# Attention block on one core: two of four x blocks by transposing DMAs, second queries projected ahead of the exps, first bound rows on VectorE, planner tables set to uniform values

## The chip, the core and the metric

The kernel runs on one core of a Trainium2 chip. The metric is device time in microseconds (us) of one execution. Three executions of the kernel before took 406.65 to 406.67 us, median 406.66 us. One core has a matrix engine (PE, with PEld its weight loads), VectorE (DVE), ScalarE (ACT), GpSimd (POOL), and SyncE (SP), which here only issues DMAs.

## The reference

```python
qkv = (x @ wqkv).reshape(B, S, 3, H, Dh).transpose(2, 0, 3, 1, 4)   # B=1 S=2048 D=448 H=16 Dh=28
scores = einsum("bhqd,bhkd->bhqk", q, k) * Dh ** -0.5
p = softmax(scores, axis=-1)
o = einsum("bhqk,bhkd->bhqd", p, v)
out = o.transpose(0, 2, 1, 3).reshape(B, S, D) @ wo                 # all bf16
```

## The kernel before, in words

**Tiles.** The 2048 rows of x are four blocks of 512. Sixteen heads are four groups of four. A window is one group with one block of queries: 16 windows, each of 16 key tiles (128 keys) by 4 heads. A tile is one head's 128 keys by 512 queries, and there are 1024 tiles of scores (L941, `emit_S`).

**Softmax work is shared.** ACT takes pairs of tiles from the two-bank tiles `PA` (L1370, one exp of 128x1024). DVE takes single tiles from the banks `PD` with a cubic in place of the exp: DU (L1145), DV (L1148), then POOL's DG (L1151), then PTD (L1164). A few tiles ("early" ones, read ahead of their turn) are copied by DVE to SG (L1077) and computed by POOL alone (L1084 to L1107). PE then multiplies by the values (L1209) into `PO`.

**Bounds.** Instead of a running maximum, each score has a bound subtracted, carried in extra rows of queries and keys: the absolute queries QP times the largest absolute key. For the first two windows (w = 0 and 1) only key block 0 is known, so their first four key tiles use rows made on chip (`bound`, L749 to L757; `PBND` says which rows POOL makes, the others are DVE's). The later key tiles need all four key blocks projected, their maxima (L593, L636), the row NK (L641), and DMAs that move the keys into place (L647) and repeat NK beside them (L658).

**Start.** Block b of x must stand transposed in XT. Blocks 0 to 2 are loaded (XS, L303) and transposed by PE (L463), then copied out of the banks (L474, L476). Block 3 comes by four transposing DMAs (L310), the first of which waits for XS of block 1. Weights are loaded by L300 (WK, from ACT's queue), L307 (WQ), L314 (WV) and padded (L426 on POOL, L427 on ACT). POOL clears VA and WO (L497, L498) ahead of L426. Queries of window 0 and keys of block 0 are projected (L720, L584), reduced, moved and bounded, and then the first exp runs. The second queries (w = 1) and the other keys are projected between the first exps.

**What sets the order.** A list scheduler inside the kernel (L1402 to L1486) simulates the five engines with durations written in the file, and emits every instruction in the order that it finds. `XLAT` and the `lat=` of the SP items tell it when loads land; `prio`, `elig` and `acq` say what goes first, when, and into which bank. `PLAN` (L45 to L69) holds one number per window for many of its choices: how many ready rows start a window's value products, how far ahead an early tile is taken, priorities of DU, DV, PTD, and when projections may start and must be done. In the kernel before these numbers differ from window to window. Each engine then runs its own list in order; a wait at the head of a list stops all that stands behind it.

Of the kernel before, what the change touches and what calls it, by code (L numbers as in the profile page):

```python
# [13 lines left out]
ALU = mybir.AluOpType  # L14
# [31 lines left out]
    "PVROWS": [8, 10, 10, 3, 6, 7, 11, 7, 7, -10, 7, 7, 11, 11, 11, 9],  # L46
    "AHEAD": [16, 9, 16, 15, 7, 10, 12, 8, 12, 13, 11, 6, 13, 7, 11, 5],
    "GCLEAR": [0.4, -0.4, -0.3, 0.3, 0.2, 0.7, 0.3, -0.1, 0.2, 1, 0.5, 1, 0.4, 0.8, 1.4, 0.1],
    "SCLEAR": [0, 1.1, 1.8, 1.7, 1.4, 0.4, 0.7, 0, 0.3, 1.5, 0.1, 0.9, 1.8, 2, 0.4, 1.8],
# [6 lines left out]
    "QBY": [64, 33, 84, 35, 80, 63, 48, 35, 70, 68, 37, 26, 24, 83, 73, 82],
    "QLEAD": [-88, 27, 38, -61, -3, -56, 48, 32, 6, -83, 0, 17, 28, -85, -90, 11],
    "KFROM": [34, 11, 29, -12, -10, -8, 19, 19, 18, 30, 41, -14, 27, 26, 8, 2],
    "KBY": [23, 12, 48, -4, 29, 50, 40, 54, 30, -2, 2, 49, 14, 48, 9, 40],
    "KLEAD": [34, 27, -74, -63, -7, -50, 32, 24, 1, -25, -43, -62, 18, -27, -8, 47],  # L60
    "VFROM": [-2, 8, 7, 30, -2, 49, 8, 15, 40, -1, -5, 24, 46, -9, 35, 43],
    "VBY": [41, 25, 52, 0, 56, 14, 11, 57, 57, 37, 59, 4, 57, -8, 17, 49],
    "VLEAD": [48, 73, 0, -21, 9, -23, 6, 54, 46, 20, 21, -27, -34, 9, -21, -1],
    "NORM": [20, 10, -10, 38, 6, 40, 20, 10, -14, -4, 9, -10, -18, 20, 32, -1],
    "TAIL": [8, 8, 40, 1],
    "PART": [-34, -19, 34, 37, -30, 40, 3, 30],
    "OUT": [0, 10, 28, 39, 20, -22, 7, -6, 5, -8, -2, 39, -30, -10, 13, 39],
    "SLK": [0.2, 0.22, 0.21, 0.19, 0.12, 0.21, 0.2, 0.12, 0.24, 0.11, 0.08, 0.22, 0.17, 0.19, 0.27, 0.12],
# [49 lines left out]
def kernel(  # L118
# [87 lines left out]
    BP2 = 34  # L206
    PBND = ((3,), (2, 3))
# [10 lines left out]
    XT3 = 14.0  # L218
    XBAR = True
# [4 lines left out]
    out_perm = out[0][QW:S].rearrange("(p t) d -> p t d", t=NKT - TPC)  # L224
    out_last = out[0][0:QW].rearrange("(t p) d -> p t d", t=TPC)
    x_perm = x2[QW:S].rearrange("(p t) c -> p t c", t=NKT - TPC)
# [6 lines left out]
    def sb(shape, dt, name):  # L233
        return const.tile(shape, dt, name=name)

    XT = [[sb([CK + 2 * hf if b < NQC - 1 else P, 2, QW], BF16, f"XT{b}_{hf}") for hf in range(2)] for b in range(NQC)]
# [15 lines left out]
    XS = [sb([P, TPC, D], BF16, f"XS{b}") for b in range(NQC - XBAR)]  # L252
# [46 lines left out]
    xs_dma = []  # L299
    nc.scalar.dma_start(out=WK[:, :, 0:GW], in_=wq3[:, :, D:D + GW])  # L300
    for b in range(NQC):
        if b < NQC - 1:
            xs_dma.append(nc.sync.dma_start(out=XS[b][:], in_=x_perm[:, b * TPC:(b + 1) * TPC, :]))  # L303
        elif not XBAR:
            nc.sync.dma_start(out=XS[b][:], in_=x2[0:QW].rearrange("(t p) c -> p t c", t=TPC))
        if b == 0:
            nc.sync.dma_start(out=WQ[:, :, 0:GW], in_=wq3[:, :, 0:GW])  # L307
    if XBAR:
        for cc in range(CC):
            r = nc.sync.dma_start(out=XT[NQC - 1][cc // 2][:, cc % 2, :],  # L310
                                  in_=bass.AP(x.tensor, x.offset + cc * CK, [[D, QW], [1, P]]), transpose=True)
            if cc == 0:
                tc.add_manual_dep(r.ins, xs_dma[1].ins.name, mybir.DependencyInfo(mybir.DependencyClass.Sync, mybir.DependencyReason.DATA))
# [122 lines left out]
    tbank = (((PD[0][:], None), (PD[1][:], None)), ((PD[2][:], None), (PA[0][:, 0:QW], None)),  # L436
             ((PO[:], None), (PD[1][:], -2)), ((PD[2][:], 2), (PO[:], 3)))
# [10 lines left out]
    for b in range(NQC - XBAR):  # L448
        xs_in = add(Op("SP", 0.01, None, prio=-2000 + b, lat=XLAT[b]))
        for hf in range(2):  # L450
            tv = tbank[b][hf][0].bitcast(BF16)

            if b == 0 and hf == 1 and XSP:
                tv2 = PA[0][:, QW:2 * QW].bitcast(BF16)
            else:
                tv2 = tv

            def tr(b=b, hf=hf, tv=tv, tv2=tv2):
                for c2 in range(2):
                    for t in range(TPC):  # L460
# [38 lines left out]
    add(Op("POOL", 1.5, clear, prio=-4900))  # L499
# [19 lines left out]
    wvin = add(Op("SP", 0.01, None, prio=-1997, lat=11.0))  # L519
# [175 lines left out]
    def task_Q(g, c):  # L695
# [9 lines left out]
        else:  # L705
# [27 lines left out]
        if w < NF:  # L733
# [7 lines left out]
            else:  # L741
# [3 lines left out]
                out=QP[n][:].bitcast(U16), in0=qb[0][:].bitcast(U16), scalar1=0x7FFF, scalar2=None, op0=ALU.bitwise_and), deps=[e0], prio=pq + 10))  # L745
            if w:
                e1 = add(Op("DVE", TS5, lambda: nc.vector.tensor_copy(out=qb[1][:], in_=qb[0][:]), deps=[e0], prio=pq + 15))

            def bound(q, i, col, deps, prio):  # L749
                st = SI[i]  # L750
                if i in PBND[w]:
# [5 lines left out]
                    scalar1=col[HP * st:HP * (st + 1), 0:1], scalar2=None, op0=ALU.mult), deps=deps, prio=prio))  # L757
# [115 lines left out]
    def task_OP(c):  # L873
# [23 lines left out]
        add(Op("SP", 0.05, lambda: nc.sync.dma_start(out=out_perm[:, c * TPC:c * TPC + n, :], in_=OUTS[c][:, 0:n, :]),  # L897
               deps=evs, prio=due))

    def late_tile(ap):  # L900
# [4 lines left out]
        nc.sync.dma_start(out=out_perm[:, c * TPC + tq:c * TPC + tq + 1, :], in_=OUTS[c][:, tq:tq + 1, :])  # L905
# [648 lines left out]
```

## Time and profile before

| what | before |
|---|---|
| time of the profiled execution | 406.66 us |
| its span | 404.9 us |
| busy: ACT, DVE, PE, POOL | 393.7, 386.0, 353.5, 347.2 us |
| first exp starts, last exp starts | 11.86, 396.4 us |
| exps on ACT (L1370) | 419, of them 418 of two tiles and one of a single tile |
| tiles on DVE with POOL's help, on POOL alone | 162, 25 |

The span is what the profiler sees of the execution; 1.8 us lie around it. "Idle before" is the time that an engine sat idle ahead of a group of instructions, with what released it. The durations of one instruction overlap its neighbours a little: DU, DV and PTD show 0.68 us each but follow one another every 0.60 us.

### The profile page before, as it was taken

The page shows a single profiled execution, that of the slowest core. Times are in us where ns is not written, and L with a number is a line of the kernel's source. Part 1 is how long each engine was busy: PE and PEld are TensorE (multiplying, and loading weights), DVE is VectorE, ACT ScalarE, POOL GpSimd, SP SyncE. Part 2 cuts the span into 40 slices and gives each one's busy share as a digit, 9 for nine tenths or more (in the row PEclk, how much of TensorE's full clock was granted, in tenths as well). Part 3 has the DMA queues.
Part 4 walks back from the last instruction along what each step waited for, and adds up shares of the span by engine and source line. Part 5 has one row for each costly group of instructions (what it writes and reads, how often), then busy time and mean ns, then how long its engine had stood idle before and what let it go on. Part 6 is the DMA issues. An engine that isn't in the chain of part 4 may idle for free.

```text
span 404.9 us, 7616 instructions
## 1 busy us (share of the span) xinstructions
PE 353.5 (87%) x2596; PEld 115.6 (29%) x2607; DVE 386.0 (95%) x696; ACT 393.7 (97%) x434; POOL 347.2 (86%) x372
## 2 busy tenths in 40 slices
PE   7999979898888888899898987898898898989896
PEld 4342332322232232322322232222223322222232
DVE  5989999999999999999999999999999999999985
ACT  5999999999999999999999999999999999999994
POOL 5429999889899889899999899988898997989990
PEclk9999999999999999999999999999999999999999
DMA  5551120212301020110411000010220001001012
GB/s 171 92 85 43 47 55 25 38 42 42 66 2 47 0 52 8 18 41 2 108 31 33 24 22 8 1 48 1 73 54 16 32 2 56 11 17 59 5 69 91
DMA packets 36446, 16.58 MB, mean 41 GB/s; under 512 B 28784, under 2 KB 33136, under 8 KB 36408
## 3 DMA queue, kind: packets, MB, share of 16 engines
q1 hardware_dynamic: 35800, 15.89, 16.2%
q8 instruction: 20, 0.33, 0.4%
q10 hardware_dynamic: 608, 0.22, 0.2%
q14 instruction: 18, 0.15, 0.1%
HBM read 7.44 MB, written 1.97 MB: 23 GB/s over the span
## 4 chain that ended last, share of the span: by engine, by line
ACT 46%; DVE 20%; PE 18%; issue 8%; POOL 7%; DVEq 0%; POOLq 0%
ACT PTA L1370 46%; PE PA L941 7%; PE PO L1209 5%; DVE DU L1145 5%; DVE PTD L1164 5%; DVE DV L1148 4%; POOL DG L1151 4%; PE PD L941 2%; PE PO L720 1%; DVE SG L1077 1%; POOL GU L1092 1%; DVE VA L815 1%; POOL OSB L1017 1%; DVE KB L622 1%; DVE QB L731 1%
## 5 line engine op out<-in xcount | busy, mean ns | idle before, releaser
L1370 ACT ACTIVATE PTA<-PA 128x1024 bf16<-128x1024 f32 x419 | 384.7, 1163 | 1.0 <-PE PA L941 0.6
L941 PE MATMUL PA<-QB,KB 64*128 64x512 bf16 x837 | 168.2, 381 | 40.6 <-ACT PTA L1370 37.5
L1151 POOL TENSOR_TENSOR DG<-DV,DU 128x512 f16<-128x512 f16 x162 | 185.4, 1156 | 16.7 <-DVE DV L1148 11.8
L941 PEld LDWEIGHTS <-KB 64*128 64x128 bf16 x1024 | 61.7, 93 | 182.4 <-issue 173.8
L1164 DVE SCALAR_TENSOR_TENSOR PTD<-PD,DG 128x512 uint16<-128x512 f32 x162 | 109.1, 680 | 3.1 <-POOL DG L1151 2.1
L1148 DVE SCALAR_TENSOR_TENSOR DV<-PD,DU 128x512 f16<-128x512 uint16 x162 | 108.0, 680 | 0.8
L1145 DVE TENSOR_SCALAR DU<-PD 128x512 f16<-128x512 uint16 x162 | 106.9, 678 | 1.9 <-PE PD L941 1.8
L1209 PE MATMUL PO<-PTA,VA 128*32 128x512 bf16 x837 | 83.1, 385 | 0.0
L941 PE MATMUL PD<-QB,KB 64*128 64x512 bf16 x187 | 68.6, 377 | 3.2 <-DVE PTD L1164 1.2
L1209 PE MATMUL PO<-PTD,VA 128*32 128x512 bf16 x187 | 53.6, 386 | 0.0
L1209 PEld LDWEIGHTS <-VA 128*32 128x32 bf16 x1024 | 18.7, 94 | 46.4 <-issue 44.9
L1092 POOL TENSOR_TENSOR GU<-GV,GU 128x512 f16<-128x512 f16 x25 | 28.9, 1156 | 2.3 <-DVE QP L768 1.6
L1090 POOL TENSOR_TENSOR GV<-GE,GU 128x512 f16<-128x512 f32 x25 | 28.9, 1158 | 1.7 <-DVE QP L768 0.8
L1094 POOL TENSOR_TENSOR SG<-SG,GU 128x512 f32<-128x512 f32 x25 | 28.9, 1157 | 1.7 <-DVE QP L768 0.8
L1044 POOL TENSOR_TENSOR OT<-OSB,RRB 128x512 bf16<-128x512 f32 x15 | 19.0, 1270 | 1.5 <-DVE PTD L1164 1.5
L1084 POOL TENSOR_SCALAR GU<-SG 128x512 f16<-128x512 uint16 x25 | 15.5, 621 | 5.1 <-DVE SG L1077 3.4
L1077 DVE COPY SG<-PD 128x512 f32<-128x512 f32 x25 | 17.1, 682 | 0.7 <-PE PD L941 0.4
L1087 POOL TENSOR_SCALAR GE<-SG 128x512 f32<-128x512 uint16 x25 | 15.5, 621 | 2.0
L720 PE MATMUL PO<-XT,WQP 112*128 112x512 bf16 (+1 forms) x52 | 16.9, 385 | 0.3 <-DVE OSB L1029 0.3
L584 PE MATMUL PO<-XT,WKP 112*128 112x512 bf16 (+1 forms) x52 | 16.9, 385 | 0.1
L800 PEld LDWEIGHTS <-XT 112*128 112x128 bf16 x256 | 13.6, 97 | 10.7 <-issue 10.5
L1107 POOL TENSOR_SCALAR PTD<-SG 128x512 uint16<-128x512 f32 x25 | 15.5, 621 | 0.9
(120 smaller groups left out, 198.1 us busy)
## 6 DMA issues: line engine op xcount, KB each, us to landing
RRB<-SCR SPq DMA_DIRECT2D x15, 256.0 KB
QB<-QP SPq DMA_DIRECT2D x56, 32.0 KB
KB<-NK SPq DMA_DIRECT2D x12, 128.0 KB
XS<-in_x_dram SPq DMA_DIRECT2D x3, 448.0 KB
QB<-QB SPq DMA_DIRECT2D x28, 32.0 KB
out_dram<-XS SPq DMA_DIRECT2D x2, 448.0 KB
KB<-KB SPq DMA_DIRECT2D x6, 128.0 KB
RRB<-SCRF SPq DMA_DIRECT2D x2, 256.0 KB
```

The costliest lines, as they stand in the source:

```text
L720: ops = chain_mm(CC, lambda cc: nc.tensor.matmul(out=ap(), lhsT=WQP[g][0:rows_of(g, c, cc), cc, :], rhs=XT[c][cc // 2][0:rows_of(g, c, cc) ...
L941: nc.tensor.matmul(out=ap, lhsT=KB[g % 2][i // 2][a:a + 64, j * P:(j + 1) * P], rhs=QB[w % NQB][i // 2][a:a + 64, :], start=True, stop=Tru ...
L1077: cp = add(Op("DVE", CPY, lambda: nc.vector.tensor_copy(out=X[:], in_=PX[slot.idx][:]), deps=[sop], prio=n - PLAN["LEADC"][now()], lat=0.165))
L1090: g3 = add(Op("POOL", PTT, lambda: nc.gpsimd.tensor_tensor(out=GV[:], in0=GE[:], in1=GU[:], op=ALU.mult), deps=[g2], prio=prio + 2, kind=" ...
L1092: g4 = add(Op("POOL", PTT, lambda: nc.gpsimd.tensor_tensor(out=GU[:], in0=GV[:], in1=GU[:], op=ALU.mult), deps=[g3], prio=prio + 3, kind=" ...
L1094: g5 = add(Op("POOL", PST, lambda: nc.gpsimd.tensor_tensor(out=X[:], in0=X[:], in1=GU[:], op=ALU.add), deps=[g4], prio=prio + 4, kind="g", ...
L1145: p1 = add(Op("DVE", P1, lambda: nc.vector.tensor_scalar(out=DU[b][:], in0=lo, scalar1=SIG / 65536, scalar2=SIG * (SS - 0.5), op0=ALU.mult ...
L1148: p2 = add(Op("DVE", P1, lambda: nc.vector.scalar_tensor_tensor(out=DV[b][:], in0=lo, scalar=65536 * (SS - 0.5 + CE / C3), in1=DU[b][:], o ...
L1151: gq = add(Op("POOL", PTT, lambda: nc.gpsimd.tensor_tensor(out=DG[b][:], in0=DV[b][:], in1=DU[b][:], op=ALU.mult), deps=[p2], prio=n, kind ...
L1164: f = add(Op("DVE", P1, lambda: nc.vector.scalar_tensor_tensor(out=PTD[st["s"].idx][:].bitcast(U16), in0=PX[slot.idx][:], scalar=EBITS + C ...
L1209: nc.tensor.matmul(out=PO[HP * st:HP * (st + 1), :], lhsT=VA[g][:, j, st, :], rhs=r["p"][i][1](), start=first, stop=last, tile_position=(0 ...
L1370: nc.scalar.activation(out=PTA[pslot.idx][:, 0:len(ns) * QW], in_=PA[s.idx][:, 0:len(ns) * QW], func=ACT.Exp, bias=ACT_BIAS, scale=ACT_SCALE)
```

## The change

Block 1 of x comes by transposing DMAs as block 3 does, so `XBAR` becomes the pair (1, 3). SP's list is now: XS of block 0, WQ, four transposes for block 1, XS of block 2, four transposes for block 3, WV. The rows of x are dealt to blocks anew (blocks 0 and 2 interleaved from row 1024 on, block 1 rows 512 to 1023, block 3 rows 0 to 511), and the output follows. Block 1 loses the two rows of ones that carried the bound's offset, so its projections are 112 rows deep and its copies add the offset column. POOL's clearing of VA and WO goes behind L426. All four first bound rows of window 0 are DVE's (`PBND`). The second queries may be projected at once into their own bank, the second keys into `PO`. The short DVE operations on QP and QB are marked as sharing a port with POOL. Every row of `PLAN` but TAIL becomes nearly uniform.

```diff
-    "PVROWS": [8, 10, 10, 3, 6, 7, 11, 7, 7, -10, 7, 7, 11, 11, 11, 9],
+    "PVROWS": [8, 10, 10, 10, 10, 10, 10, 10, 10, 10, 10, 10, 9, 9, 9, 6],
...
-    BP2 = 34
-    PBND = ((3,), (2, 3))
+    BP2 = 20
+    PBND = ((), (2, 3))
...
-    XT3 = 14.0
-    XBAR = True
+    XTL = {1: 9.0, 3: 14.5}
+    XBAR = (1, 3)
+    XTR = {1: QW, 3: 0}
+    XTP = {0: 0, 2: TPC}
...
-    for b in range(NQC):
-        if b < NQC - 1:
-            xs_dma.append(nc.sync.dma_start(out=XS[b][:], in_=x_perm[:, b * TPC:(b + 1) * TPC, :]))
...
-            if cc == 0:
-                tc.add_manual_dep(r.ins, xs_dma[1].ins.name, mybir.DependencyInfo(mybir.DependencyClass.Sync, mybir.DependencyReason.DATA))
+    nc.sync.dma_start(out=XS[0][:], in_=x_perm[:, XTP[0]:XTP[0] + TPC, :])
+    nc.sync.dma_start(out=WQ[:, :, 0:GW], in_=wq3[:, :, 0:GW])
+    for b in XBAR:
         for cc in range(CC):
+            nc.sync.dma_start(out=XT[b][cc // 2][:, cc % 2, :],
+                              in_=bass.AP(x.tensor, x.offset + XTR[b] * D + cc * CK, [[D, QW], [1, P]]), transpose=True)
+        if b == 1:
+            nc.sync.dma_start(out=XS[2][:], in_=x_perm[:, XTP[2]:XTP[2] + TPC, :])
     nc.sync.dma_start(out=WV[:], in_=wq3[:, :, 2 * D:3 * D])
...
-    tbank = (((PD[0][:], None), (PD[1][:], None)), ((PD[2][:], None), (PA[0][:, 0:QW], None)),
-             ((PO[:], None), (PD[1][:], -2)), ((PD[2][:], 2), (PO[:], 3)))
+    tbank = (((PD[0][:], None), (PD[1][:], None)), ((PD[2][:], None), (PO[:], None)),
+             ((PD[1][:], -2), (PD[0][:], -3)), ((PD[2][:], 2), (PO[:], 3)))
...
-    add(Op("POOL", 1.5, clear, prio=-4900))
+    add(Op("POOL", 1.9, clear, prio=-4900, elig=lambda t: ("k", 0) in w_ready and w_ready[("k", 0)].start is not None))
...
-    wvin = add(Op("SP", 0.01, None, prio=-1997, lat=11.0))
+    wvin = add(Op("SP", 0.01, None, prio=-1997, lat=17.0))
...
-    k0_bank = [PD[0][:], PD[0][:], PD[1][:], PO[:]]
-    k0_wait = [lambda: [xt_half[0]], lambda: kuse[0], lambda: [xt_half[5]], lambda: [xt_half[4]]]
+    k0_bank = [PD[0][:], PO[:], PD[1][:], PD[0][:]]
+    k0_wait = [lambda: [xt_half[0]], lambda: [], lambda: [xt_half[4]], lambda: [xt_half[5]]]
...
                 task = {"slot": d_slots[2]}
-                acq = lambda t: xt_half[2].done(t)
+                acq = lambda t: True
```

More of the change, by code (lines that the diff above doesn't have):

```diff
@@ L56 @@
[L56 to L62, printed above, removed]
@@ L63 @@
-    "VLEAD": [48, 73, 0, -21, 9, -23, 6, 54, 46, 20, 21, -27, -34, 9, -21, -1],
-    "NORM": [20, 10, -10, 38, 6, 40, 20, 10, -14, -4, 9, -10, -18, 20, 32, -1],
+    "PVROWS": [8, 10, 10, 10, 10, 10, 10, 10, 10, 10, 10, 10, 9, 9, 9, 6],
+    "AHEAD": [10, 10, 10, 10, 10, 10, 10, 10, 10, 10, 10, 10, 10, 10, 10, 10],
+    "GCLEAR": [0.5, 0.5, 0.5, 0.5, 0.5, 0.5, 0.5, 0.5, 0.5, 0.5, 0.5, 0.5, 0.5, 0.5, 0.5, 0.5],
+    "SCLEAR": [1, 1, 1, 1, 1, 1, 1, 1, 1, 1, 1, 1, 1, 1, 1, 1],
[3 rows of a table added]
+    "LEADC": [10, 10, 10, 10, 10, 10, 10, 10, 10, 10, 10, 10, 10, 10, 10, 10],
@@ new lines @@
+    "PVMORE": [2, 2, 2, 2, 2, 2, 2, 2, 2, 2, 2, 2, 2, 2, 2, 2],
+    "QFROM": [0, 0, 0, 0, 0, 0, 0, 0, 0, 0, 0, 0, 0, 0, 0, 0],
+    "QBY": [60, 60, 60, 60, 60, 60, 60, 60, 60, 60, 60, 60, 60, 60, 60, 60],
+    "QLEAD": [0, 0, 0, 0, 0, 0, 0, 0, 0, 0, 0, 0, 0, 0, 0, 0],
+    "KFROM": [0, 0, 0, 0, 2, 2, 2, 2, 2, 2, 2, 2, 2, 2, 2, 2],
+    "KBY": [0, 0, 0, 0, 30, 30, 30, 30, 30, 30, 30, 30, 30, 30, 30, 30],
+    "KLEAD": [0, 0, 0, 0, 0, 0, 0, 0, 0, 0, 0, 0, 0, 0, 0, 0],
+    "VFROM": [0, 0, 0, 0, 4, 4, 4, 4, 4, 4, 4, 4, 4, 4, 4, 4],
@@ L65 @@
+    "VBY": [0, 0, 0, 0, 32, 32, 32, 32, 32, 32, 32, 32, 32, 32, 32, 32],
+    "VLEAD": [0, 0, 0, 0, 0, 0, 0, 0, 0, 0, 0, 0, 0, 0, 0, 0],
+    "NORM": [-10, -10, -10, -10, -10, -10, -10, -10, -10, -10, -10, -10, -10, -10, -10, -10],
     "TAIL": [8, 8, 40, 1],
-    "PART": [-34, -19, 34, 37, -30, 40, 3, 30],
-    "OUT": [0, 10, 28, 39, 20, -22, 7, -6, 5, -8, -2, 39, -30, -10, 13, 39],
-    "SLK": [0.2, 0.22, 0.21, 0.19, 0.12, 0.21, 0.2, 0.12, 0.24, 0.11, 0.08, 0.22, 0.17, 0.19, 0.27, 0.12],
+    "PART": [0, 0, 0, 0, 0, 0, 0, 0],
@@ L69 @@
+    "OUT": [0, 0, 0, 0, 0, 0, 0, 0, 0, 0, 0, 0, 0, 0, 0, 0],
+    "SLK": [0.2, 0.2, 0.2, 0.2, 0.2, 0.2, 0.2, 0.2, 0.2, 0.2, 0.2, 0.2, 0.2, 0.2, 0.2, 0.2],
 }
@@ L223 @@
     x2 = x[0]
-    out_perm = out[0][QW:S].rearrange("(p t) d -> p t d", t=NKT - TPC)
-    out_last = out[0][0:QW].rearrange("(t p) d -> p t d", t=TPC)
-    x_perm = x2[QW:S].rearrange("(p t) c -> p t c", t=NKT - TPC)
+    out_perm = out[0][2 * QW:S].rearrange("(p t) d -> p t d", t=2 * TPC)
+    out_rows = {b: out[0][XTR[b]:XTR[b] + QW].rearrange("(t p) d -> p t d", t=TPC) if b in XBAR else out_perm[:, XTP[b]:XTP[b] + TPC, :]
+                for b in range(NQC)}
+    out_last = out_rows[NQC - 1]
+    x_perm = x2[2 * QW:S].rearrange("(p t) c -> p t c", t=2 * TPC)
     wq3 = wqkv.rearrange("(cc p) n -> p cc n", p=CK)
@@ L234, in sb @@
         return const.tile(shape, dt, name=name)
-    XT = [[sb([CK + 2 * hf if b < NQC - 1 else P, 2, QW], BF16, f"XT{b}_{hf}") for hf in range(2)] for b in range(NQC)]
+    XT = [[sb([CK + 2 * hf if b not in XBAR else P, 2, QW], BF16, f"XT{b}_{hf}") for hf in range(2)] for b in range(NQC)]
     WK = sb([CK, CC, GW], BF16, "WK")
@@ L251 @@
     OT = [[sb([P, QW], BF16, f"OT{g}_{c}") for c in range(NQC)] for g in range(G)]
-    XS = [sb([P, TPC, D], BF16, f"XS{b}") for b in range(NQC - XBAR)]
+    XS = [sb([P, TPC, D], BF16, f"XS{b}") for b in range(NQC - 1)]
     PTA = [sb([P, UA * QW], BF16, f"PTA{i}") for i in range(NPA)]
@@ L359 @@
         nc.gpsimd.tensor_tensor(out=bndcol[pr][:], in0=bndcol[pr][:], in1=mcol[:], op=ALU.add)
-    for b in range(NQC - 1):
+    for b in XTP:
         nc.scalar.activation(out=XT[b][1][UB:CK + 2, 1, :], in_=zrow[UB:CK + 2, :], func=ACT.Identity, bias=1.0, scale=1.0)
@@ L447 @@
         add(Op("PE", MM, lambda: warm(n), prio=5000, kind="K", elig=lambda t: 4.6 < t < 9, acq=lambda t: warm_open[0]))
-    for b in range(NQC - XBAR):
+    for b in XTP:
         xs_in = add(Op("SP", 0.01, None, prio=-2000 + b, lat=XLAT[b]))
@@ L466 @@
                          elig=None if 2 * b + hf < 2 + TE else lambda t: len(k0mm) == 2 * CC and all(o.end is not None for o in k0mm),
-                         acq=None if tbank[b][hf][1] is None else (lambda t, k=tbank[b][hf][1]: (quse and quse[1].done(t)) if k < 0 else xt_half[k].done(t))))
+                         acq=None if tbank[b][hf][1] is None else (lambda t, k=tbank[b][hf][1]: (quse and quse[1].done(t)) if k == -2 else (0 in kuse and all(o.done(t) for o in kuse[0])) if k == -3 else xt_half[k].done(t))))
             eng = "DVE" if hf == 0 else HENG[b]
@@ L486 @@
             xt_half[2 * b + hf] = evo
-    if XBAR:
-        xt_done[NQC - 1].append(add(Op("SP", 0.01, None, prio=-1996, lat=XT3)))
-        add(Op("SP", 8.5, None, prio=-1995.5))
+    for b in XBAR:
+        xt_done[b].append(add(Op("SP", 0.01, None, prio=-1996, lat=XTL[b])))
+    add(Op("SP", 13.0, None, prio=-1995.5))
     def load_wo():
@@ L559, in chain_mm @@
         return ops
-    k0_bank = [PD[0][:], PD[0][:], PD[1][:], PO[:]]
-    k0_wait = [lambda: [xt_half[0]], lambda: kuse[0], lambda: [xt_half[5]], lambda: [xt_half[4]]]
+    k0_bank = [PD[0][:], PO[:], PD[1][:], PD[0][:]]
+    k0_wait = [lambda: [xt_half[0]], lambda: [], lambda: [xt_half[4]], lambda: [xt_half[5]]]
     def unit_rows(g, sc):
-        return sc < NQC - 1 and (g > 0 or sc > 0)
+        return sc in XTP and (g > 0 or sc > 0)
     def rows_of(g, sc, cc):
@@ L744, in task_Q @@
             ab = add(Op("DVE", TS5, lambda: nc.vector.tensor_scalar(
-                out=QP[n][:].bitcast(U16), in0=qb[0][:].bitcast(U16), scalar1=0x7FFF, scalar2=None, op0=ALU.bitwise_and), deps=[e0], prio=pq + 10))
+                out=QP[n][:].bitcast(U16), in0=qb[0][:].bitcast(U16), scalar1=0x7FFF, scalar2=None, op0=ALU.bitwise_and), deps=[e0], prio=pq + 10, kind="sb"))
             if w:
-                e1 = add(Op("DVE", TS5, lambda: nc.vector.tensor_copy(out=qb[1][:], in_=qb[0][:]), deps=[e0], prio=pq + 15))
+                e1 = add(Op("DVE", TS5, lambda: nc.vector.tensor_copy(out=qb[1][:], in_=qb[0][:]), deps=[e0], prio=pq + 15, kind="sb"))
             def bound(q, i, col, deps, prio):
@@ L756, in bound @@
                     out=q[i // 2][HP * (st ^ 1):HP * ((st ^ 1) + 1), :], in0=QP[n][HP * st:HP * (st + 1), :],
-                    scalar1=col[HP * st:HP * (st + 1), 0:1], scalar2=None, op0=ALU.mult), deps=deps, prio=prio))
+                    scalar1=col[HP * st:HP * (st + 1), 0:1], scalar2=None, op0=ALU.mult), deps=deps, prio=prio, kind="sb"))
             for i in range(HG):
@@ L832 @@
     task_Q(0, 0)
-    open_when(a_slots[0], [xt_half[3]])
+    open_when(a_slots[0], xsp)
     a_slots[1].free_at = 0.0
-    open_when(d_slots[0], kuse[1])
+    open_when(d_slots[0], kuse[3])
     open_when(d_slots[1], kuse[2])
-    open_when(o_slot, kuse[3])
+    open_when(o_slot, kuse[1])
     for jq in range(NQC):
@@ L896, in task_OP @@
         n = len(evs)
-        add(Op("SP", 0.05, lambda: nc.sync.dma_start(out=out_perm[:, c * TPC:c * TPC + n, :], in_=OUTS[c][:, 0:n, :]),
+        add(Op("SP", 0.05, lambda: nc.sync.dma_start(out=out_rows[c][:, 0:n, :], in_=OUTS[c][:, 0:n, :]),
                deps=evs, prio=due))
```

16 lines of the change are left out of this document (1 added, 15 removed), and 6 rows, old and new, of the table PLAN.

## The prediction

> **What bounds the kernel now.** I read busy shares and costliest groups first.
>
> ```profile
> PE 353.5 (87%) x2596; PEld 115.6 (29%) x2607; DVE 386.0 (95%) x696; ACT 393.7 (97%) x434; POOL 347.2 (86%) x372
> ...
> L1370 ACT ACTIVATE PTA<-PA 128x1024 bf16<-128x1024 f32 x419 | 384.7, 1163 | 1.0 <-PE PA L941 0.6
> ```
>
> ACT is full. Its exps are busy 384.7 us and sat idle 1.0 us in all, 0.6 of it ahead of the first. 384.7 / 419 = 0.918 us each. So the time is: start of the first exp (11.86) + the exps + the way from the last exp to the end (404.9 - 397.0 = 7.9). Between, only a stall of ACT or another number of exps can count. DVE is nearly as full: 2 more tiles moved from ACT to DVE would save one exp, 0.918.
>
> What sets 11.86 is read in the timelines of POOL, PE, DVE and ACT over the first 12 us.
>
> ```profile
> 4.92 1.60 POOL L498 MEMSET WO<- 128x1792 bf16 x1
> 6.46 0.56 POOL L426 COPY WKP<-WK 112x448 bf16<-112x448 bf16 x1
> ```
> ```profile
> 7.08 0.61 PE L584 MATMUL PD<-XT,WKP 112*128 112x512 bf16 x2 [1.36 <-POOL WKP L426]
> ...
> 11.45 0.37 PE L941 MATMUL PA<-QB,KB 64*128 64x512 bf16 x1 [0.36 <-DVE QB L755]
> ```
> ```profile
> 10.38 1.02 DVE L755 TENSOR_SCALAR QB<-QP,KPART 32x512 bf16<-32x512 bf16 x1
> ```
> ```profile
> 11.86 1.02 ACT L1370 ACTIVATE PTA<-PA 128x1024 bf16<-128x1024 f32 x1 [0.61 <-PE PA L941]
> ```
>
> The reader is to see two delays. POOL clears WO ahead of the key weights, so PE starts the keys at 7.08, while their x has been copied since 5.99 (5.30 + 0.69). And the second bound row takes 1.02 beside POOL's row (10.14 to 11.25), where the first took 0.34; the first pair of scores waits for it. Last, SP's timeline:
>
> ```profile
> 1.66 0.97 SPq L303 DMA_DIRECT2D XS<-in_x_dram  x2
> 7.12 5.13 SPq L310 DMA_TRANSPOSE XT<-in_x_dram  x4
> 12.30 0.58 SPq L314 DMA_DIRECT2D WV<-in_wqkv_dram  x1
> ```
>
> Four transposes hold SP for 5.13 us: 1.28 each, against 0.45 for a plain load.
>
> **Part 1, the start.** *Weights:* L426 goes ahead of the clears, so at 4.74, when POOL's column work ends (WK left on its own queue at 0.74, WQ, issued later, was in use at 5.16), at the latest at 5.2. Either way it ends by 5.8, before DVE's copy at 5.99. PE starts at 6.05, not 7.08: -1.03. The clears are hidden: POOL has nothing until the rows of w = 1. *Rows:* four on DVE without POOL beside them, 0.34 to 0.36 each, so the second one is not held for 0.68. Together the first pair of scores could go at 9.7 instead of 11.45, an exp at 10.2.
>
> *But the built order of the changed kernel puts other work ahead of that pair on PE:* two products of the second queries (half 0 of block 1), eight transposes of XS of block 2, two more products (half 1 of block 1). All wait for DMAs that SP issues in turn: XS0 at 0.74, WQ at 1.20, four transposes from 1.66 to 6.79, and only then XS of block 2, at 6.84 instead of 2.2. Block 1 itself is early enough. In the DMA view of 7.6 to 11.6 us (0.1 us a digit) the first transpose of before, issued at 7.12, is the burst from 8.4 to 9.3, and the others follow 1.3 apart:
>
> ```profile
> DMA  1000000005359998510003495799961000479249
> ```
>
> So a transpose lands 2.2 behind its issue, and the fourth, issued at 5.5, at 7.7. Block 2 is the gate. How long does a load of 448 KB take? Lower: 1.0 to its first packet (issue 0.74, first traffic at 1.75 in the view below), 1.65 for the bytes (two of them pass between 4.2 and 7.5), 0.5 to the engine: 10.0. Upper: XS0 itself, issued at 0.74, used by PE at 4.62, 3.88 later: 10.7.
>
> ```profile
> DMA  0009909590167514687996798599699899899799
> ```
>
> (the DMA view of 1.6 to 3.6 us, 0.05 us a digit.) I take R = 10.45, between the two, and keep 9.9 to 10.9. [...] From R: eight transposes 0.45 (8.81 to 9.26), two products 0.45, the pair to its exp 0.41 (11.45 to 11.86). First exp at R + 1.31 = 11.76, **-0.1 us** (-0.65 to +0.35). What was saved on POOL and DVE is thus cover for a new wait on block 2.
>
> **Part 2, the first thirty us.** Removed from between the exps: four query products and the copies of block 1 (two of 0.67 on DVE, sixteen transposes 0.9 on PE, ahead of the first exp before). Key tiles from the fifth on need NK. Before:
>
> ```profile
> 18.75 2.52 SPq L647 DMA_DIRECT2D KB<-KB  x4
> 21.47 2.67 SPq L658 DMA_DIRECT2D KB<-NK  x4
> ```
> ```profile
> 26.04 0.47 POOL L989 COPY FW<-KB 128x16 bf16<-128x16 bf16 x3 [1.11 <-DMA KB<-NK]
> ```
>
> The last repeat is visible at 26.04, 1.9 after its issue ended, and exp 17 read it just then (11.86 + 16 x 0.918 = 26.5). In the new order DVE's list up to NK, with its durations from Q1's copy at 11.4 on (eleven of 0.6 to 0.75, three short ones, two rows beside POOL at 1.02 and 0.36), ends at about 20.0 instead of 21.44, its key copy at 18.2 instead of 18.73; SP then issues 4 x 0.63 + 4 x 0.67 to 23.5, visible at 25.4. But DVE has its first tile ahead of exp 4, so the fifth key tile is met in exp 15, not 16, and the last of the four heads in exp 17 at 25.5 + 0.4. Margin about zero: **+0.2** (0 to 0.8). No other part of the startup can hold ACT: block 3's transposes are issued 7.33 to 12.46 (before to 12.25), WV at 12.5 (12.30).
>
> **Part 3, the count.** In the built order ACT has 419 exps of two tiles, where one had a single tile: **+0.46** (half of 0.918). DVE has 163 tiles for 162, POOL alone 23 for 25. DVE's sum: + 3 x 0.60 - 2 x 0.60 (SG) - 2 x 0.60 (block 1) + 6 copies with the offset column (0.743 for 0.680, 0.06 each) + one row 0.36 = +0.1. Same load. POOL has 10 us less (two chains of 3 x 0.62 + 3 x 1.16). It was not the bound.
>
> **Part 4, the uniform plan.** The trace of before can't show it; the order can. Positions of projections are no tighter (queries of each window from the third on done 14 to 40 exps ahead, before 12 to 42). Keep-alive matmuls of zeros, placed where PE has nothing, are 54 for 38 into PO, never more than two per exp: no long gap is planned. Summing DVE's spacings along its list from each tile's start to the freeing of the bank that PE needs next, there are 8 places with no margin, before 2. PE's waits on PTD were 1.2 us in 5 times (0.24 each), and at most 0.4 us reached ACT, a third. 8 x 0.24 / 3 = 0.6, less the 0.2 of the old two: **+0.4**; bounds 0 (PE waits for ACT 37.5 us in all, which is slack) and 1.9 (all eight in full).
>
> **Part 5, the end.** TAIL is unchanged, PE has 12 value products behind the last pair for 23, and the chain through DVE to the last store is the same: 0.
>
> Sum: -0.1 + 0.2 + 0.46 + 0.4 = +0.96. Span 404.9 + 0.96 = 405.9, with the 1.8 around it 407.6. The profiled execution took 406.66, the median itself.
>
> **Rivals.**
> 1. *Block 2 lands early; not slower.* The kernel's own table has it at 8.9. If R is 8.9, the pair goes at 9.8, the exp at 10.2: 406.66 - 1.65 + 0.46 + 0.2 (the rest) = 405.7. It decides from R = 9.5 down (sum zero). For it: the wire is idle between the bursts above, so XS would not queue behind the transposes' bytes. Against: SP's 1.28 each is issue time, and 6.84 plus any load seen here passes 9.9.
> 2. *The uniform plan stalls ACT.* All eight places in full and the keys late by their upper end: 406.66 - 0.1 + 0.8 + 0.46 + 1.9 = 409.7; with R at its upper end 410.2. For: DVE is 95% full, so a lag is caught up slowly. Against: the evenly spread fillers.
> 3. *PE's clock falls in the new wait.* PE idles from about 8.45 to 10.45. The eight warm-up matmuls at the start took 3.56 us, 0.44 each, where later ones follow every 0.22. Another such stretch would lose half of 3.56, 1.8 us of PE's work, just where keys and scores share it: 407.6 + 1.8 = 409.4. The rows against it: the granted clock stayed 1.00 over the idle 5.7 to 7.08, and fell only behind the last matmul, which ended at 401.3, in
>
> ```profile
> 404.00:404.90 0.90, 0.00 (x0) 0.00 (x0) 0.00 (x0) 0.00 (x0) 0.00 (x0) 0.52 0.00 0
> ```
>
>    some 2.7 us later; 2.0 us of idle is less. [...]
> 4. *The change doesn't do what it says* for the queries: they stand ahead of the exps in the order, so no.
>
> **Chances.** Forecast (406.6 to 408.8) 0.58; rival 1 0.14; rival 2 0.20; rival 3 0.08. Range 405.9 to 410.2: down to rival 1, up to rival 2's upper end. About 0.2% (0.8 us) is what a measurement can tell from none. Faster takes rival 1: 0.14. The forecast straddles 407.47, 0.28 of it within. So same 0.28, slower 0.58.
>
> **What would show it.** PE's eight transposes of block 2 with a wait for DMA of about 2 us, first exp near 11.8; L426 at 4.8; SP's XS near 6.8; one ACT idle near 25; ACT's total idle 1.5 to 2. It is wrong if the first exp starts by 10.8 or after 12.5, or if ACT idles over 3 us behind it.

## The result, and the profile after

The changed kernel takes 407.83 us (median of 20 executions, 406.92 to 409.6), the kernel before 406.66 (20 executions): a ratio of 1.003, interval 1.0022 to 1.0038. It is 1.2 us slower. Its profiled execution took 407.58 with a span of 405.8, for 406.66 and 404.9 before. Its executions fall into two groups by their mean granted PE clock: ten at 1.000 (median 407.5) and ten at 0.991 to 0.996 (median 408.3). Experiments 1 and 2 show why.

ACT is still the full engine (from the page of after: busy times, and the exps with the idle time ahead of them):

```profile
PE 361.7 (89%) x2606; PEld 116.4 (29%) x2606; DVE 385.8 (95%) x696; ACT 393.4 (97%) x433; POOL 336.4 (83%) x360
...
L1368 ACT ACTIVATE PTA<-PA 128x1024 bf16<-128x1024 f32 x419 | 384.8, 1151 | 2.3 <-PE PA L939 2.3
```

The exps are busy as long as before (384.8 for 384.7), POOL lost 11 us that nobody misses, and ACT's wait for scores grew from 1.0 to 2.3. Where it waits is read in ACT's timeline (start, length, group, idle before):

```profile
12.61 12.94 ACT L1368 ACTIVATE PTA<-PA 128x1024 bf16<-128x1024 f32 x14 [1.81 <-PE PA L939]
25.72 1.02 ACT L1368 ACTIVATE PTA<-PA 128x1024 bf16<-128x1024 f32 x1 [0.17 <-PE PA L939]
27.03 8.39 ACT L1368 ACTIVATE PTA<-PA 128x1024 bf16<-128x1024 f32 x9 [0.29 <-PE PA L939]
35.79 362.51 ACT L1368 ACTIVATE PTA<-PA 128x1024 bf16<-128x1024 f32 x395
```

1.81 of it lies ahead of the first exp, 0.46 near 26, where the late key tiles begin, and from 35.79 on ACT runs 395 exps without one listed wait. So the loss is at the start. POOL and DVE did there what the change asks of them:

```profile
5.14 0.56 POOL L424 COPY WKP<-WK 112x448 bf16<-112x448 bf16 x1 [0.41 <-DMA WK<-in_wqkv_dram]
```
```profile
9.55 1.48 DVE L753 TENSOR_SCALAR QB<-QP,KPART 32x512 bf16<-32x512 bf16 x4
```

The key weights are padded at 5.14 instead of 6.46, and the four rows take 0.37 each and end at 11.03; the first two, all that the first pair needs, are done at 10.3. PE's timeline shows what ate that lead:

```profile
4.76 1.52 PE L461 MATMUL PD<-ident,XS 128*112 128x128 bf16 x12
...
8.37 0.59 PE L718 MATMUL PD<-XT,WQP 112*128 112x512 bf16 x2
11.13 0.65 PE L461 MATMUL PD<-ident,XS 128*112 128x128 bf16 x8 [2.17 <-DMA XS<-in_x_dram]
11.62 0.60 PE L718 MATMUL PD<-XT,WQP 112*128 112x512 bf16 x2
12.15 0.39 PE L939 MATMUL PA<-QB,KB 64*128 64x512 bf16 x2
```

The first scores (L939) stand in PE's list behind block 2's transposes (L461), and these wait 2.17 us for a load that SP issued late:

```profile
1.66 5.12 SPq L308 DMA_TRANSPOSE XT<-in_x_dram  x4
6.83 0.58 SPq L311 DMA_DIRECT2D XS<-in_x_dram  x1
```

The profiles are split in the same way below: start of the first exp, from there to the end of the last one, from there to the end of the span. Left out are the first profile of experiment 4, in which the clock fell later on, and those of experiment 7, whose loss lies in the middle.

| profiled execution of | first exp | exps | end | span |
|---|---|---|---|---|
| before | 11.86 | 385.42 | 7.6 | 404.9 |
| after | 12.61 | 385.69 | 7.5 | 405.8 |
| after, second profile (e10) | 12.98 | 386.20 | 7.5 | 406.7 |
| after, third profile (e11) | 12.26 | 385.50 | 7.5 | 405.3 |
| after with PE kept busy (e1) | 12.14 | 385.39 | 7.5 | 405.0 |
| after, block 2 loaded first (e2) | 10.40 | 386.09 | 7.5 | 404.0 |
| after, block 2 planned late (e12) | 10.40 | 387.29 | 8.4 | 406.1 |
| before with the uniform plan (e4) | 11.86 | 385.21 | 8.7 | 405.8 |
| before, clears moved (e9) | 11.33 | 385.41 | 7.6 | 404.3 |
| before, clears and row moved (e6) | 10.43 | 385.87 | 7.6 | 403.9 |

After against before: +0.75 at the start, +0.27 in the exps, -0.1 at the end.

### The profile page after: what moved, and what is told of

Same layout as the page of the kernel before. It is cut to its first block, busy times and chain, and to the rows that moved or that the text cites. A ratio compares the mean times of both kernels' runs of the same rounds, so it can differ in the third digit from the quotient of the medians.

```text
span 405.8 us, 7607 instructions
## 1 busy us (share of the span) xinstructions
PE 361.7 (89%) x2606; PEld 116.4 (29%) x2606; DVE 385.8 (95%) x696; ACT 393.4 (97%) x433; POOL 336.4 (83%) x360
## 4 chain that ended last, share of the span: by engine, by line
ACT 38%; DVE 28%; PE 17%; issue 7%; POOL 6%; DMA 2%; SPq 1%; DVEq 0%; POOLq 0%
ACT PTA L1368 38%; DVE DU L1143 7%; DVE DV L1146 7%; DVE PTD L1162 7%; PE PA L939 6%; PE PO L1207 6%; POOL DG L1149 4%; PE PD L939 2%; SPq L308 1%; DVE SG L1075 1%; DMA XS<-in_x_dram 1%; DVE OSB L1027 1%; PE PD L881 1%; DVE VA L813 1%; DVE KB L620 1%
## 5 line engine op out<-in xcount | busy, mean ns | idle before, releaser
L1368 ACT ACTIVATE PTA<-PA 128x1024 bf16<-128x1024 f32 x419 | 384.8, 1151 | 2.3 <-PE PA L939 2.3
L939 PE MATMUL PA<-QB,KB 64*128 64x512 bf16 x838 | 170.4, 381 | 31.7 <-ACT PTA L1368 29.7
L939 PEld LDWEIGHTS <-KB 64*128 64x128 bf16 x1024 | 62.8, 93 | 178.8 <-issue 170.7
L939 PE MATMUL PD<-QB,KB 64*128 64x512 bf16 x186 | 68.7, 378 | 2.4 <-DVE PTD L1162 1.6
L1092 POOL TENSOR_TENSOR SG<-SG,GU 128x512 f32<-128x512 f32 x23 | 26.6, 1155 | 1.4 <-DVE QP L766 0.8
L1088 POOL TENSOR_TENSOR GV<-GE,GU 128x512 f16<-128x512 f32 x23 | 26.6, 1157 | 1.1
L1090 POOL TENSOR_TENSOR GU<-GV,GU 128x512 f16<-128x512 f16 x23 | 26.5, 1153 | 0.6 <-DVE QP L766 0.3
L1329 PE MATMUL PO<-zrow,zeros 128*128 128x512 bf16 x54 | 18.7, 386 | 0.1
L1082 POOL TENSOR_SCALAR GU<-SG 128x512 f16<-128x512 uint16 x23 | 14.2, 618 | 5.4 <-DVE SG L1075 3.9
L718 PE MATMUL PO<-XT,WQP 112*128 112x512 bf16 (+1 forms) x56 | 18.5, 385 | 0.0
L1075 DVE COPY SG<-PD 128x512 f32<-128x512 f32 x23 | 15.7, 681 | 2.1 <-PE PD L939 2.1
L798 PE MATMUL PO<-WV,XT 112*128 112x112 bf16 x208 | 15.6, 214 | 0.4 <-DVE KB L620 0.3
```

Source lines behind the costliest of these rows:

```text
L798: nc.tensor.matmul(out=ap()[:, jj * GW:(jj + 1) * GW], lhsT=XT[jq][cc // 2][0:CK, cc % 2, jj * P:(jj + 1) * P], rhs=WV[:, cc, g * GW:(g + ...
L939: nc.tensor.matmul(out=ap, lhsT=KB[g % 2][i // 2][a:a + 64, j * P:(j + 1) * P], rhs=QB[w % NQB][i // 2][a:a + 64, :], start=True, stop=Tru ...
L1075: cp = add(Op("DVE", CPY, lambda: nc.vector.tensor_copy(out=X[:], in_=PX[slot.idx][:]), deps=[sop], prio=n - PLAN["LEADC"][now()], lat=0.165))
L1088: g3 = add(Op("POOL", PTT, lambda: nc.gpsimd.tensor_tensor(out=GV[:], in0=GE[:], in1=GU[:], op=ALU.mult), deps=[g2], prio=prio + 2, kind=" ...
L1090: g4 = add(Op("POOL", PTT, lambda: nc.gpsimd.tensor_tensor(out=GU[:], in0=GV[:], in1=GU[:], op=ALU.mult), deps=[g3], prio=prio + 3, kind=" ...
L1092: g5 = add(Op("POOL", PST, lambda: nc.gpsimd.tensor_tensor(out=X[:], in0=X[:], in1=GU[:], op=ALU.add), deps=[g4], prio=prio + 4, kind="g", ...
```

## The experiments

The theory after the result: block 2's late load holds the start, and in half of the executions PE's clock falls in that wait. The rivals: the uniform plan costs the time, or the new work ahead of the exps does.

**1. Keep PE busy in the wait.** Nine matmuls of zeros go behind the last product ahead of block 2.

```diff
+        if w == 1:
+            prev1 = ops[1].fn
+            def warm_wait():
+                prev1()
+                for _ in range(9):
+                    nc.tensor.matmul(out=PO[:], lhsT=zeros[:], rhs=zrow[:], start=True, stop=True)
+            ops[1].fn = warm_wait
```

> The changed kernel with nine matmuls of zeros into PO while PE waits for block 2 (2.2 us in the trace after). Theory (the wait on block 2 leaves PE idle, and in the executions with a mean granted clock of 0.991 to 0.996 the clock fell behind it for one stretch or two): the granted clock is 1.00 in nearly all executions, the spread of 406.9 to 409.6 shrinks to below 408, and the median falls from 407.8 to 407.4 to 407.6; the first exp stays at 12.6, since the matmuls fill only the wait. Rival (the clock falls for another reason, as where in the start the clock rises): clock, spread and median stay, 407.8 plus up to 0.2 for matmuls that outlast the wait.

Measured: 407.29 (11 executions, 406.58 to 407.4), mean clock 0.999 to 1.000 in each. The upper group of after is gone. The first exp came at 12.14 and not at 12.6, since block 2 came earlier, at 10.66. From PE's timeline:

```profile
8.17 2.11 PE L727 MATMUL PO<-zrow,zeros 128*128 128x512 bf16 x9
10.66 0.65 PE L461 MATMUL PD<-ident,XS 128*112 128x128 bf16 x8 [0.39 <-DMA XS<-in_x_dram]
```

Matmuls that compute nothing make the median 0.5 us better. The undisturbed half of after's executions is 0.3 better than all of them (407.5 for 407.83), so of the 1.2 us of loss 0.3 is the clock's by that count; the other 0.2 that this kernel gains is not explained.

**2. Two more profiles of after**, to see the low clock itself.

> The kernel after once more, for its profile. If the granted clock falls at the start in this execution (about every second one by the clocks of the runs), it is halved for one stretch of 3.4 us that begins near 11, after the wait on block 2: block 2's eight transposes take about 0.95 instead of 0.65, the two products behind them 1.06 instead of 0.60, and the first exp comes at 13.2 to 13.5, the time is near 408.3. If it does not fall: first exp at 12.5 to 12.7, time near 407.5. If the low clock of the other runs lies elsewhere, the first exp is at 12.6 and the profile has a low stretch in the middle or at the end.

> The same kernel and the same question again, since either case is had in about half of the executions.

Both cases came: 408.46 (e10) and 407.07 (e11), each with a first exp 0.2 earlier than expected. In the windows view of e10 (1 us each; busy time of PE, PEld, DVE, ACT and POOL with counts, then granted clock, DMA share, GB/s):

```profile
11.00:12.00 1.00, 1.00 (x10) 0.47 (x8) 0.00 (x0) 0.00 (x0) 0.00 (x0) 0.65 0.97 172
12.00:13.00 1.00, 1.00 (x4) 0.21 (x3) 0.58 (x1) 0.01 (x1) 0.00 (x0) 0.50 0.49 87
13.00:14.00 1.00, 1.00 (x4) 0.18 (x4) 1.00 (x5) 1.00 (x1) 0.00 (x0) 0.50 0.73 111
14.00:15.00 1.00, 1.00 (x10) 0.91 (x12) 0.23 (x2) 0.94 (x2) 0.62 (x1) 0.64 0.51 98
```

A mean of 0.65 is 0.30 us at full and 0.70 at half clock, so it fell at 11.30; 0.64 is 0.72 at half clock, so it rose at 14.72: 3.42 us. PE and ACT of e10 in that time:

```profile
10.82 0.70 PE L461 MATMUL PD<-ident,XS 128*112 128x128 bf16 x8 [2.56 <-DMA XS<-in_x_dram]
11.32 1.06 PE L718 MATMUL PD<-XT,WQP 112*128 112x512 bf16 x2
```
```profile
12.98 2.10 ACT L1368 ACTIVATE PTA<-PA 128x1024 bf16<-128x1024 f32 x2 [2.88 <-PE PA L939]
```

Block 2 came at 10.82, even ahead of the first profile's 11.13, but the two products took 1.06 instead of 0.60 and the first exp was 2.16 behind it, not 1.48. In e11 block 2 came at 10.78 and the clock held: first exp at 12.26, 0.72 earlier.

Which case came went with the wait in these profiles. PE's busy time in the 3.41 us that end at the fall in e10, and in the 3.41 us up to the same place of PE's list in the first profile (with counts, then granted clock, DMA share, GB/s):

```profile
7.89:11.30 3.41, 0.85 (x10) 1.00 0.94 197
```
```profile
8.20:11.61 3.41, 1.24 (x12) 1.00 1.12 206
```

In e10 these 3.41 us hold the wait of 2.56 and 0.85 us of matmuls, and the clock falls at their end. In the first profile they hold the wait of 2.17 and 1.24 us of matmuls, and the clock held. There are two other profiles with this list at the start. With the plan of before (experiment 7, e5) the wait of 2.30 ended at 10.75 and the clock fell at 10.93; in e11 the wait was 2.00 and the clock held. So it fell behind the two longer waits and held behind the two shorter ones. In the two profiles in which it held, block 0's first twelve transposes had taken longer (1.52 in the first profile and 1.49 in e11, for 0.83 in e10 and 0.88 in e5) and the wait began later (8.96 and 8.78, for 8.26 and 8.45). Whether the wait's length decides or its place, four profiles don't tell. The ends of the kernels, where PE idles for good, give no one distance either: the fall comes 2.7 us behind the last matmul in before (at 404.03) and 3.3 in the first profile of after (at 405.71).

**3. Block 2's load ahead of the transposing ones**, nothing else:

```diff
+    nc.sync.dma_start(out=XS[2][:], in_=x_perm[:, XTP[2]:XTP[2] + TPC, :])
     for b in XBAR:
...
-        if b == 1:
-            nc.sync.dma_start(out=XS[2][:], in_=x_perm[:, XTP[2]:XTP[2] + TPC, :])
```

> The changed kernel with the load of block 2 issued ahead of block 1's four transposing DMAs; nothing else moves. Theory (PE's wait for block 2, behind four transposes of 1.28 us on SP, sets the first exp): block 2 is there before PE asks for it, PE's 2.17 us wait goes, the pair of scores waits for the key copies on ACT (done 10.1) and the first exp starts at 10.7 to 11.2 instead of 12.61; time 405.9 to 406.5. Rival A (the fourth transpose of block 1, 0.6 us later, takes its place): first exp 11.2 to 11.8, time 406.5 to 407.0. Rival B (the start is not what the time hangs on, the uniform plan is): first exp earlier but the time within 0.3 of 407.8, with ACT idle later on.

Measured: 406.31 (11 executions, 405.78 to 406.8, clock 1.0), ratio to before 0.9992 (0.9983 to 1.0). From PE and ACT of this kernel:

```profile
8.86 0.61 PE L460 MATMUL PD<-ident,XS 128*112 128x128 bf16 x8 [0.49 <-ACT QB L735]
```
```profile
10.40 3.77 ACT L1367 ACTIVATE PTA<-PA 128x1024 bf16<-128x1024 f32 x4 [0.19 <-PE PA L938]
```

Block 2 no longer waits for a DMA (what is left is its bank, read by L735), and the first exp starts at 10.40, 2.2 earlier, a little better than expected. One moved line brings back 1.5 us of 407.83, or 1.2 of the undisturbed 407.5, and the clock held in all eleven executions: the place of this load in SP's list is the loss of the change. 0.4 is given back in the exps, where three small waits are listed up to 25.2.

**4. The same loads, but the planner is told that block 2 lands late.**

```diff
-    XLAT = (4.6, 7.3, 8.9, 9.6)
+    XLAT = (4.6, 7.3, 11.2, 9.6)
```

> The kernel after with one number changed: the planner is told that block 2 lands at 11.2 instead of 8.9 (XLAT). The loads are unchanged, so block 2 still lands near 11. In the built order PE now has the first two pairs of scores, and the products of the second keys and queries, ahead of the eight transposes of block 2. Theory (the start is late only because the first pair stands in PE's list behind a wait for block 2): the first exp goes when the bound rows are done, at 10.6 to 11.0 instead of 12.61; block 2's transposes still start at 11.1 and cost ACT nothing, since two exps cover them. Time 407.5 - 1.7 + up to 0.5 given back in the plan = 405.8 to 406.3. Rival (the loads themselves, or the work for the second keys, hold the start whatever the order): first exp at 12 or later, or a gap of over 1 us behind the first two exps; time 407 or more.

> The kernel with the late table entry once more, for a profile without the clock's fall at 269. Its first exp is at 10.6, 2.0 ahead of after, and yet its undisturbed executions take 407.9 to 408.5. If the new built order gives it back by stalls, ACT's waits on scores behind the first exp sum to 1.5 us or more; if by the end, the way from the last exp to the end of the span is 8.5 or more, for 7.5; both may be.

Measured: 408.48 (6 executions, 407.87 to 412.07), and 407.89 for the second profile. The start did as the theory says: first exp at 10.59 and 10.40, though block 2's transposes still began at 11.24 in the first profile. The time did not, and both of its expected leaks are there. From the second profile, the copy behind the last value products:

```profile
400.07 0.53 ACT L902 CAST XS<-PA 128x448 bf16<-128x448 f32 x1 [2.38 <-PE PA L901]
```

It waits 2.38, for 1.46 in after: the end is 8.4 long. The exps' stretch is 1.6 longer, of which 0.7 are waits (four listed, 1.1 in sum, for two with 0.5 in after). Most of the rest shows as busy time of the exps, 385.6 for 384.8, but the exps are no slower: in both kernels an exp mostly ends 0.917 behind the one before it. An exp lasts longer than that (1.16 us on average here) and overlaps the one before, so one that comes late by less than the overlap lists no wait and adds busy time. Thirteen exps come over 0.05 late, for five in after, and all lateness in sum is 1.6 more than there. What each of them waited for was not followed. One number in the table for the start re-lays all that follows, since the list scheduler places each operation after the one before. In its first profile the clock also fell, from 269.3 to 279.5 (412.07).

**5. The uniform plan in the kernel before**: `PLAN` of after, nothing else.

> The kernel before with the uniform planner tables of the changed one, and nothing else. Its order has 419 exps of two tiles. Theory (the count costs 0.46, the plan's stalls 0.4 or less): 407.1 to 407.6, first exp at 11.86 as before, ACT idle 0.4 to 1.0 us behind it. Rival (the uniform plan is the whole of the 1.17 us): 407.8 or more. Second rival (the plan costs nothing): 406.7.

Measured: 407.6 (12 executions, one at 410.57 with the clock at 0.996, the others within 407.57 to 407.68), ratio 1.0027 (1.0014 to 1.0039). It costs 0.94, within the theory's range but not as stalls. ACT's one listed wait behind the first exp is 0.22, where before has none, and the last exp ends 0.2 earlier, though half an exp is added. The end is 1.1 longer:

```profile
399.55 0.53 ACT L904 CAST XS<-PA 128x448 bf16<-128x448 f32 x1 [2.49 <-PE PA L903]
```

This copy waited 1.33 before; in the run with the uniform plan, behind its last pair of scores PE has 40 value products left (L1209), for 24 before: they run until 398.65 instead of 397.7. The plan leaves a backlog, and it is paid at the end, where no exp covers it. In after PE has 16 left, and the end is no longer.

**6. Part 1 in the kernel before.** First the clears alone, behind L426:

```diff
-    add(Op("POOL", 1.5, clear, prio=-4900))
+    add(Op("POOL", 1.5, None, prio=-4900))
...
+        if nm == "k":
+            pad_k = w_ready[(nm, 0)].fn
+            w_ready[(nm, 0)].fn = lambda: (pad_k(), clear())
```

> The kernel before with POOL's clears behind the key weights' padding and nothing else: the move of Part 1 alone, without the fourth bound row on DVE. Theory (two delays in a row, 1.03 by the clears and 0.68 by POOL's row beside DVE's second): the keys start at 6.0 instead of 7.1, but the second bound row is still 1.0 long, so the first exp goes at 10.9 to 11.1 (11.86 - 0.7 to - 1.0) and the time is 405.7 to 406.0. Rival (the two delays are one: what is gained on the keys is lost on the rows, or the queries become the later input): first exp at 11.5 or later, time 406.4 or more.

Then also POOL's row of window 0 on DVE, right behind DVE's third:

```diff
...
+                if w == 0 and i == 2:
+                    return add(Op("DVE", 0.36, lambda: (row(2), row(3))[1], deps=deps, prio=prio))
+                if w == 0 and i == 3:
+                    return add(Op("POOL", 1.25, None, deps=deps, prio=prio, lat=0.157))
```

> The kernel before, with two parts of the change alone: the clearing of VA and WO stands behind the padding of the key weights, and the fourth bound row of window 0 is made by VectorE; every other instruction keeps its place. Theory (POOL's clear and POOL's row are the two delays that bound the first exp): keys projected from 6.05 to 6.2 instead of 7.08, second row in 0.35 instead of 1.02, first exp at 10.2 to 10.6, time 405.0 to 405.5. Rival A (the sixteen transposes of block 2, whose load lands at 8.3 or so, hold PE ahead of the scores): first exp 10.8 to 11.2, 405.7 to 406.1. Rival B (keys from the fifth tile on, or block 3, come no earlier, so what is won is given back as ACT idle near 25): 406.3 to 406.7.

Measured: 406.04 (11 executions, ratio 0.9983, 0.9975 to 0.9992) for the clears, 405.8 (9 executions, 405.29 to 405.85, ratio 0.9975, 0.9966 to 0.9984) for both. DVE's rows with the clears moved alone, and then with both:

```profile
9.48 1.79 DVE L758 TENSOR_SCALAR QB<-QP,KPART 32x512 bf16<-32x512 bf16 x3
```
```profile
9.24 0.72 DVE L767 TENSOR_SCALAR QB<-QP,KPART 32x512 bf16<-32x512 bf16 x2
9.99 0.71 DVE L756 TENSOR_SCALAR QB<-QP,KPART 32x512 bf16<-32x512 bf16 x2
```

Three rows take 1.79 while POOL makes the fourth, four take 1.46 when it does not. First exp at 11.33 and 10.43: two delays in a row, as read from the profile of before, though the clears alone gave 0.5 of the 0.7 to 1.0 expected (block 0's twelve transposes took 1.53 in that profile, for 0.86 before). With both, the first exp came as the theory says, but the time missed its 405.0 to 405.5: the span gains 1.0 of the 1.4 at the start, since the second pair now waits for a bank that block 1's transposed half holds until DVE copies it:

```profile
11.47 0.61 PE L953 MATMUL PA<-QB,KB 64*128 64x512 bf16 x4 [0.59 <-DVE XT L474]
```

This is the fastest kernel of the study, 0.9 us faster than before: the small edits of Part 1 without the transposing loads.

**7. The plan of before in the kernel after**, as it is (e5) and with block 2 loaded first (e7).

> The kernel after with the PLAN of before: the structure alone. With the run of before under the uniform plan this makes the square of plan and start. Forecast theory (plan: half an exp more, 0.46, and some stalls, up to 0.4): 418 exps of two tiles for 419 of after, first exp still at 12.6 since PE's list at the start is the same; time 407.5 - 0.5 to - 0.9 = 406.6 to 407.0, with the same spread by the granted clock. Rival (the old plan was fitted to the old start and does not fit this one): no gain or a loss, 407.4 or more, with ACT's waits on scores in the middle above 2 us.

> The kernel after with block 2's load ahead of the first transposing transfers, and the PLAN of before. If plan and start add up: 406.3 (the load first under the uniform plan) - 0.5 to - 0.9 = 405.4 to 405.8, first exp 10.4. If the old plan does not fit the new start: 406.3 or more, with the first exp still at 10.4 and the time lost behind it.

Measured: 429.92 (4 executions, ratio 1.0574) and 427.14 (4 executions, ratio 1.0508): worse than either theory had it, by far, and on the rival's side. The first exps start as expected (13.17, with the clock fallen; 10.38). From ACT and PE of e5:

```profile
122.47 6.52 ACT L1368 ACTIVATE PTA<-PA 128x1024 bf16<-128x1024 f32 x7 [10.86 <-PE PA L939]
```
```profile
117.29 0.95 PE L798 MATMUL PO<-WV,XT 112*128 112x112 bf16 x16
118.07 0.38 PE L1323 MATMUL PD<-zrow,zeros 128*128 128x512 bf16 x1
118.95 1.02 PE L718 MATMUL PO<-XT,WQP 112*128 112x512 bf16 x4 [0.50 <-DVE VA L813]
```

At one place PE's list has the keys, values and queries of a coming window one behind the other, each waiting for DVE to empty a bank, and no scores between: ACT stands still for 10.86, half of the 20 us by which the exps' stretch is longer than in after (405.9 for 385.7); waits of 2.61, 2.33 and 1.06 follow. The numbers of that plan go with the built order of the old start and not with this one. So the square of plan and start does not add up: the uniform plan in place of the old one costs 0.94 in the old start and saves 22 in the new, and what the uniform plan "costs" in after can't be had by putting the old one back.

## Why the prediction was right and wrong

407.6 was said, 407.83 measured, slower as forecast. But that the number fits is in part luck: the start cost 0.85 more than said and the plan about 1.0 less, and the two met in the middle.

- **Part 1, the start: -0.1 said, +0.75 in the profile; the term that failed in size.** The mechanism was right: the lead of POOL and DVE is cover for a new wait on block 2, with PE's list behind it, and SP issues the load at 6.83, as said. R was taken as 10.45; it is 11.13, 10.82 and 10.78 in the three profiles of after, the first above the upper bound of 10.9. XS0's 3.88 from issue to use, my upper row, was no upper bound: this load took 4.0 to 4.3. Its first bytes pass at 8.04, 1.2 behind the start of the issue (1.0 said) and, as for XS0, 0.6 behind its end; its last pass by 10.7 in the first profile: 2.7 for the bytes, where 1.65 was said, with block 3's transposes among them from 9.5 on. The second piece, R + 1.31, is R + 1.48. With 12.61 and 12.98 for the first exp in two of three profiles, one of the signs of being wrong, "after 12.5", came true. Experiment 3 confirms the cause: with the load first the exp starts at 10.40.
- **Part 2, the keys: +0.2 said; about +0.5, within its 0 to 0.8.** In the rhythm of 0.917 the sixteenth exp would end at 27.39; it ends at 28.05, 0.66 late, where before is 0.2 late there. PE waited 0.15 for the repeat of NK at 25.31, and ACT 0.17 and 0.29 near 26. The chain was timed too early: NK was ready at 21.31 (20.0 said), and SP issued its repeats until 25.42 (23.5 said):

```profile
22.75 2.67 SPq L656 DMA_DIRECT2D KB<-NK  x4
```

- **Part 3, the count: +0.46 said; +0.43.** The single-tile exp of before was the last one. The last two exps of before, then of after:

```profile
395.53 1.74 ACT L1370 ACTIVATE PTA<-PA 128x1024 bf16<-128x1024 f32 x2
```
```profile
396.13 2.17 ACT L1368 ACTIVATE PTA<-PA 128x1024 bf16<-128x1024 f32 x2
```

  The other half of the last exp is 2.17 - 1.74 = 0.43.
- **Part 4, the plan: +0.4 said; about -0.6 between the exps: the term that failed in sign.** ACT has no listed wait behind 35.8. The eight places without margin, read from the order, cost ACT nothing, and rival 2 did not come. What Part 4 did not ask is what the old plan cost. Behind ACT's copy of RR at 35.97, before ran to its last exp as this line shows:

```profile
36.45 360.83 ACT L1370 ACTIVATE PTA<-PA 128x1024 bf16<-128x1024 f32 x393
```

  After ran 395 exps in 362.51, all of two tiles. Two more exps and the other half of the last are 1.83 + 0.43 = 2.26; the stretch grew by 1.68, so 0.6 of small delays is gone. Before with the uniform plan ran its 395 in 362.38, 0.7 less, so it is the plan that saves them, in the old start too. There the plan still costs 0.94, at the end of the kernel, where I had not looked for it (experiment 5).
- **Part 5, the end: 0 said, -0.1.** Right, though the way from the last exp to the end is 7.6 before and not 7.9: that exp ends at 397.28.
- **Rival 3, the clock: chance 0.08 said; it came in about half of the executions.** It adds 0.8 between the two groups (1.4 between e10 and e11: 0.7 to the first exp, 0.7 to the exps behind it), not the 1.8 that the rival was priced at. The argument against it failed: the idle 5.7 to 7.08 of before was 1.4 us, and the fall at 404, 2.7 us behind the last matmul, was read as "2.0 is less than 2.7". In e5 the clock fell at 10.93, behind a wait of 2.30, so 2.7 us of idle are no threshold. Experiments 1 and 2 show that the wait brought the low clock.
- **Rival 1** needed block 2 at 9.5 or earlier. It never came so; experiment 3 is that rival built by hand, and its 406.31, with 0.9983 to 1.0, is hardly a gain over before, where the rival had 405.7.

Parts 2 to 4 make +0.3 together, near the table's +0.27. Without the clock's falls the profile accounts for 407.5; with them the median is 407.83.

What stays open: what the late exps of e12 wait for, and what lets the clock fall.

## What to carry to other kernels

When a step takes a load off one engine's list, look what stands ahead of the next use in the in-order queues: here four transposing DMAs of 1.28 us of issue each stood ahead of a plain load of 0.58, and moving one line was worth 1.5 us. PE's wait of 2.0 to 2.6 us at the start cost twice, once as the wait and, in half of the executions, again as half clock behind it; nine matmuls of zeros removed the second cost. A table of numbers fitted to one built order is part of that order: change the start, and test structure and table separately in both directions before one is blamed for the other.

## What the runs showed of the hardware that was not expected

The low clock does not last equally long: in e10 it stayed at 0.50 for 3.42 us (from 11.30), in e5 for 3.41 (from 10.93) and later for 13.65 (126.98 to 140.64), in the first profile of experiment 4 for 10.24 (269.30 to 279.54). Nor does it come a fixed time behind PE's work: at the end it fell 2.7 us behind the last matmul in before and 3.3 in after.

The clock can fall without a long wait. In e5, in the 3.41 us ahead of the fall at 126.98, PE was busy 1.84 (nine matmuls), and no wait was longer than 0.52. Between 132 and 140 it stayed low though PE is listed as busy all the time. The listed busy time of the 3.41 us ahead does not decide alone: in the first profile of experiment 4 the clock fell behind 2.09 us of it (longest wait 1.32), and in the first profile of after it held behind 1.24 (8.20 to 11.61). What lets the clock fall, and what brings it back, these runs do not settle.
